# An attention block's output on one Trainium2 core: its second block by seven products, its loads ahead of the row sums' load, a fourth tile of the last head added by DMA

## The chip, the cores and the metric

The kernel runs on one core of one Trainium2 chip. The metric is the device time of one execution in microseconds; below 2% the comparison is made on medians of repeated runs. One execution was recorded by the hardware profiler.

## The reference

The inputs are one sequence of 2048 tokens of 1024 numbers (float32). Two branches see the same x and are mixed by a gate per token:

```python
qkv = (x @ wqkv).reshape(B, S, 3, H, Dh).transpose(2, 0, 3, 1, 4)   # H = 32, Dh = 32
scores = einsum("bhqd,bhkd->bhqk", q, k) * Dh ** -0.5
o = einsum("bhqk,bhkd->bhqd", softmax(scores), v)
a = o.transpose(0, 2, 1, 3).reshape(B, S, D) @ wo                    # S = 2048, D = 1024
b = ...            # experts picked by top-1 of two key tables, 64 experts, mixed by act * v
out = g * a + (1 - g) * b,    g = sigmoid((x * gate_w).sum(-1))
```

## The kernel before

The program first makes Q and K (kept in DRAM), the second branch's activations (ATD) and V. Then a loop runs over the 32 heads, 16 key tiles each. For a pair of key tiles TensorE makes the scores into a ring of PSUM banks (`scores`, L1322), ScalarE takes their exponentials into tiles P of 128 x 2048 (L1332), and TensorE multiplies the pair before with V (`pv`, L1343).

**Row sums.** The softmax needs the sum of P over all keys. `presum` adds the 16 tiles of a head: most of them by VectorE into ACC (L1370, L1372), some by DMA: one tile is written straight into ACCD, and others are added to it by an accumulating DMA on POOL's queue (L1365). `SUMS` names these key tiles; the first number is the tile that becomes ACCD. `merge` (L1375) adds ACCD to ACC. For the last head, number 31, tiles 14 and 15 are added by nobody: `rowsum` multiplies each with ones on TensorE (L1356), together with ACC, into one PSUM bank. That merge is planned at key tile 13 of the last head, ahead of the sum of tile 13.

**Normalisation.** `norm_sums` copies the sums out of PSUM and sends them to DRAM (SMD). `load_r` brings the sums of four heads back as a tile rr; `norm_r` takes the reciprocal, multiplies with the gate G64 and sends the factors to DRAM (RD). `load_rb` broadcasts them to 128 partitions (RB). `load_o` brings the unnormalised output of the heads (OD) as a tile V. Chunk 7 of each block, that is heads 28 to 31, has to wait for this chain behind the last head; chunks 0 to 6 have their factors before.

**Output.** It is made in 8 blocks of 256 tokens, each with four PSUM banks of 128 x 512. Every operand is split into a high and a low half, and three of the four half products are made. Blocks 0 and 1 are done plainly: `wo_mm` (L1525) makes 8 chunks of 12 matmuls, and `av_mm` (L1532) adds the second branch with 8 matmuls. Blocks 2 to 7 go through `unit`: seven products P1 to P7 of 12 matmuls each (L965) after Strassen and Winograd, on sums of the activations (S1 to S4, made by VectorE at L947 and split at L95 and L96) and sums of the weights (T1 to T4, prepared early and held in DRAM as TD). `load_t(i)` brings T(i+1); `Halves.operand` makes and splits one operand, `scale_o` applies the factors (L1579), `split_o` does so for the plain path (L1594), `plain_out` copies four banks and stores them.

**What sets the order.** The program is written out by hand and each engine runs its own list in order: a waiting instruction holds everything behind it on its engine or queue. The plain loads and stores are issued by SP (all from L77), the accumulating ones by POOL. Buffers are shared by name: z0, z1, wo_raw, acc, accd and V are taken again when their last reader is through. Block 0 starts with chunk 0 right behind the last head, then come the row sums, then chunks 1 to 7.

```python
1602 wo_mm(pa, 0, [0], True, False)
1603 finish(H - 1)
1604 sm = pso.tile([128, 512], F32, name="o")
1605 list(rowsum(sm, *(P[H - 1, NT - i] for i in (1, 2)), ACC.pop(H - 1)))
```

Of the kernel before, what the change touches and what calls it, by code (L numbers as in the profile page):

```python
# [16 lines left out]
S = 2048  # L17
D = 1024
H = 32
# [12 lines left out]
def gated_mha_peer_kernel(ctx, tc, xT, wqkv, wv, wo, wq, k12, ug, v, out):  # L32
# [42 lines left out]
    def dma(dst, src, queue=nc.sync):  # L75
        a, b = (ap.bitcast(F32) if ap.dtype == F32R else ap for ap in (dst, src))
        return queue.dma_start(a, b)  # L77
# [1270 lines left out]

    SUMS = (1, 3, 8, 12), (2, 4, 6)

    def rowsum(ps, *srcs):
        for src in srcs:
            for qc in range(NQ):
                yield nc.tensor.matmul(ps[32 * qc:32 * qc + 32, :], ones,  # L1356
                                       src[:, qc * 512:(qc + 1) * 512],
                                       start=(src is srcs[0]), stop=(src is srcs[-1]))

    def presum(h, kt):  # L1360
        sums = SUMS[h == H - 1]
        if kt == 0 or kt == sums[0] or (h == H - 1 and kt >= NT - 2):
            return
        if kt in sums:
            nc.gpsimd.dma_start(ACCD[h], P[h, kt], accum_op=OP.add)  # L1365
            return
        if kt == 1 + (sums[0] == 1):
            if h > 0:
                ACC[h] = wk.tile([128, S], F32, name="acc")
            nc.vector.tensor_add(ACC[h], P[h, 0], P[h, kt])  # L1370
        else:
            nc.vector.tensor_add(ACC[h], ACC[h], P[h, kt])  # L1372
# [10 lines left out]
    def finish(h):  # L1383
        g, j = divmod(h, 4)
        o = wk.tile([128, 512], F32, name="osb")
        nc.scalar.activation(o, O.pop(h), AF.Copy)
        dma(OD[:, :, j, :, g, :].rearrange("q d n s -> (q d) n s"),
            o.rearrange("p (n s) -> p n s", n=2))
# [14 lines left out]
    def norm_r(g):  # L1403
        r = R.pop(g)
        nc.vector.reciprocal(r, r)
        nc.vector.tensor_mul(r, r, G64)
        dma(RD[:, :, g, :].rearrange("j n (q m) -> (j n) q m", m=64), r)


    OC, RB = {}, {}  # L1410
# [13 lines left out]
    def load_chunk(n, k0, k1, queue=nc.sync):  # L1424
        load_o(n, k0, k1, queue)
        load_rb(n, k0, k1, queue=queue)
# [23 lines left out]
    def at(step, f, *a):  # L1450
        todo.setdefault(step, []).append((f, a))
# [14 lines left out]
            at(base + 7, load_v, g + 1, j)  # L1466
    for i, step in enumerate((6, 7, 9, 11)):
        at((H - 1) * NT + step, split_first, i)
    at((H - 1) * NT + 13, merge, H - 1)
    for k in range(2 * KC):  # L1470
        c = slice(k % 2 * D // 2, (k % 2 + 1) * D // 2)
        at((8 + k) * NT + 11, dma, raw_wo(k // 2)[:, c], wo_rows[:, :, k // 2 * D:(k // 2 + 1) * D][:, :, c])
# [9 lines left out]
    for b0 in range(0, (H + 1) * NT, BT):  # L1482
# [9 lines left out]
        for k in range(b0, b0 + BT):  # L1492
            for f, a in todo.pop(k, []):
                f(*a)
            if now:
                presum(*now[k - b0])
    assert not todo
    pss.close()
    pools["left"].close()
    pools["right"].close()  # L1500
# [15 lines left out]
    def load_at(n):  # L1516
        AT[n] = fin.tile([128, W], F32R, name="at", bufs=3)
        dma(AT[n], ATD[:, n * W:(n + 1) * W])
# [56 lines left out]
    def scale_o(n):  # L1575

        for k in range(2):
            o = OC[n][:, k * HC:(k + 1) * HC]
            nc.vector.tensor_mul(o, o, RB[n][:, k * HC:(k + 1) * HC])  # L1579
        ht.rows(OC[n])  # L1580
# [16 lines left out]
    def banks4():  # L1597
        return {(i, half): bank() for i in range(W // 128) for half in range(2)}
# [2 lines left out]
    pa = banks4()  # L1601
    wo_mm(pa, 0, [0], True, False)
    finish(H - 1)
    sm = pso.tile([128, 512], F32, name="o")
    list(rowsum(sm, *(P[H - 1, NT - i] for i in (1, 2)), ACC.pop(H - 1)))
    split_hi(1)
    for kc in range(1, KC - 1):
        split_hi(kc + 1)
        if kc == 1:
            norm_sums(H - 1, sm, nc.scalar)  # L1610
            load_r(G - 1)
            for n in range(2):
                load_at(n)
            load_o(1, 0, KC - 1)
            pso.close()
        split_lo(kc)
        wo_mm(pa, 0, [kc], False, False)
        if kc == HC:
            norm_r(G - 1)
    for n in range(2):  # L1620
        load_chunk(n, KC - 1, KC)
    load_rb(2, 0, KC)
    split_lo(KC - 1)
    split(woh[0], wol[0], raw_wo(0))

    load_t(2, None, [fin.tile([128, S], F32R, name="t3l")])
    OH[1] = zp.tile([128, KC, W], F32R, name="z1")
    OL[1] = wk.tile([128, KC, W], F32R, name="acc")  # L1630
    split_o(1, 0, HC)
    split_o(0, KC - 1, KC)
    load_o(2, 0, KC)
    load_t(0, *([keep.tile([128, S], F32R, name=f"wo_raw{j}")] for j in range(2)))
    ps_odd = Pool("ps_odd", space=PSUM)
    for (i, half), ps in pa.items():
        av_mm(0, i, half, ps)
    wo_mm(pa, 0, [KC - 1], False, True)
    split_o(1, HC, KC)
    load_at(2)  # L1640
    load_t(2, [zp.tile([128, S], F32R, name="z0")], None)
    load_t(1, *([keep.tile([128, S], F32R, name=f"wo_raw{2 + j}")] for j in range(2)))
    load_rb(3, 0, KC)
    load_o(3, 0, KC)
    pa1 = banks4()
    wo_mm(pa1, 1, list(range(KC - 1)), True, False)
    for (i, half), ps in pa1.items():
        av_mm(1, i, half, ps)
    plain_out(0, pa)
    load_t(3, *([part[k][:, 512:] for k in range(HC)] for part in (woh, wol)))  # L1650
    ht.places(wk.tile([128, S], F32R, name="acc"), "A11", "A12")
    ht.places(fin.tile([128, S], F32R, name="s31"), "S3", "S1")
    scale_o(2)
    for name in ("A11", "S3", "S1", "A12"):
        ht.operand(name)
    wo_mm(pa1, 1, [KC - 1], False, True)
    ht.places(zp.tile([128, S], F32R, name="z1"), "S2")
    ht.places(wk.tile([128, S], F32R, name="acc"), "S4", "A22")
    load_at(3)
    ht.b.update({f"B{i + 1}{j + 1}": [[part[i * HC + k][:, j * 512:(j + 1) * 512] for k in range(HC)]  # L1660
                                    for part in (woh, wol)] for i in range(2) for j in range(2)})

    def osb():
        return wk.tile([128, 512], F32, name="osb")

    def unit(n):
# [12 lines left out]

        p1 = ht.product("P1")  # L1680
        c1 = osb()
        nc.scalar.activation(c1, p1, AF.Copy)
        if n == 2:
            ht.operand("S2")
            plain_out(1, pa1)
            for name in ("S4", "A22"):
                ht.operand(name)
        if n + 2 < S // W:
            load_chunk(n + 2, 0, KC)
            load_at(n + 2)  # L1690
        ahead("A11")
        p7 = ht.product("P7")
# [10 lines left out]
        def c11():  # L1703
            p2 = ht.product("P2", lambda ps: av_mm(n, 0, 0, ps, first=True))
            pieces = 2 if last else 1
            for i in range(pieces):
                c = slice(i * 512 // pieces, (i + 1) * 512 // pieces)
                tt(c1[:, c], c1[:, c], p2[:, c])
                store(n, 0, 0, c1, c)
# [12 lines left out]
        def c21():  # L1722
            p4 = ht.product("P4", lambda ps: av_mm(n, 1, 0, ps, first=True))
            tt(u3, u3, p4)
            store(n, 1, 0, u3)

        if not last:
            c11()
# [12 lines left out]
    ps_even.close()  # L1741
    fin.close()
# [32 lines left out]
```

## Time and profile before

| | us |
|---|---|
| median of 3 runs | 1822.76 (1822.64 to 1823.33) |
| the profiled execution | 1822.43 |
| its span in the trace | 1820.6 |
| between the two, around the span | 1.8 |
| TensorE busy | 1813.5 |

The loop over heads ends near 1641 us after the span's start; from there the output runs to 1817. A line of the chain in order of time reads: start, duration, engine, tile, source line, number of instructions. A line of the timeline also names tiles and shapes, and in brackets the idle time before it with what ended it. A row of the windows gives, for a stretch, each engine's busy time and number of instructions, then the granted TensorE clock (1.00 is full), the share of the DMA engines' time and GB/s. In the page's last part the number behind the size is the median time from issue to landing. DVE is VectorE, ACT ScalarE, POOL GpSimd, SPq the queue that issues most transfers.

### The profile page before, as it was taken

The page shows a single profiled execution, that of the slowest core. Times are in us where ns is not written, and L with a number is a line of the kernel's source. Part 1 is how long each engine was busy: PE and PEld are TensorE (multiplying, and loading weights), DVE is VectorE, ACT ScalarE, POOL GpSimd, SP SyncE. Part 2 cuts the span into 40 slices and gives each one's busy share as a digit, 9 for nine tenths or more (in the row PEclk, how much of TensorE's full clock was granted, in tenths as well). Part 3 has the DMA queues.
Part 4 walks back from the last instruction along what each step waited for, and adds up shares of the span by engine and source line. Part 5 has one row for each costly group of instructions (what it writes and reads, how often), then busy time and mean ns, then how long its engine had stood idle before and what let it go on. Part 6 is the DMA issues. An engine that isn't in the chain of part 4 may idle for free.

```text
span 1820.6 us, 26391 instructions
## 1 busy us (share of the span) xinstructions
PE 1813.5 (100%) x10077; PEld 1100.2 (60%) x10077; DVE 1461.6 (80%) x1258; ACT 1313.0 (72%) x1716; POOL 227.7 (13%) x351
## 2 busy tenths in 40 slices
PE   9999999999999999999999999999999999999999
PEld 6777777788888644444444444444444444447887
DVE  8865966789967888888888888888888888897674
ACT  6545544522333699999999999999999999994221
POOL 1222222244101100000000000000000000000000
PEclk9999999999999999999999999999999999999999
DMA  7888698660267778777778878888787778866641
GB/s 272 281 276 273 216 295 289 196 220 13 81 231 247 223 166 183 156 170 165 169 171 174 185 160 179 171 172 181 164 185 167 163 164 181 186 149 240 256 157 58
DMA packets 117072, 345.23 MB, mean 190 GB/s; under 512 B 16112, under 2 KB 49552, under 8 KB 96016
## 3 DMA queue, kind: packets, MB, share of 16 engines
q1 hardware_dynamic: 87752, 196.35, 36.6%
q0 software_dynamic: 27888, 145.00, 34.5%
q10 hardware_dynamic: 1304, 2.17, 0.3%
q8 instruction: 80, 1.31, 0.3%
q14 instruction: 48, 0.39, 0.1%
HBM read 171.76 MB, written 72.36 MB: 134 GB/s over the span
## 4 chain that ended last, share of the span: by engine, by line
PE 99%; DMA 0%; ACT 0%; SPq 0%; DVE 0%; issue 0%; DVEq 0%; ACTq 0%
PE ring L1322 29%; PE o L1343 26%; PE bk L303 15%; PE pa L965 6%; PE bk L965 6%; PE bk L726 5%; PE pa L1525 2%; PE bk L984 2%; PE bk L291 2%; PE bk L342 2%; PE ring L1356 1%; PE pa L1532 1%; PE bk L191 0%; DMA xh<-in_xT 0%; PE bk L359 0%; ACT P L1332 0%
## 5 line engine op out<-in xcount | busy, mean ns | idle before, releaser
L1332 ACT ACTIVATE P<-ring 128x1024 f32<-128x1024 f32 (+2 forms) x1031 | 913.0, 984 | 13.3 <-DMA accd<-P 0.2
L1372 DVE TENSOR_TENSOR acc<-acc,P 128x2048 f32<-128x2048 f32 x319 | 730.9, 2291 | 74.4 <-ACT P L1332 47.9
L1343 PE MATMUL o<-P,V 128*32 128x512 f32 x3840 | 464.9, 599 | 0.0
L1322 PE MATMUL ring<-Q,K 98*128 98x512 f32 x1024 | 271.8, 407 | 0.1
L1322 PE MATMUL ring<-z,z 98*128 98x512 f32 x1020 | 270.5, 407 | 0.6 <-ACT accd L1332 0.6
L1322 PEld LDWEIGHTS ring<-Q,K 98*128 98x128 f32 x1024 | 182.4, 188 | 143.5 <-ACT P L1332 73.6
L1322 PEld LDWEIGHTS ring<-z,z 98*128 98x128 f32 x1020 | 181.7, 188 | 142.1 <-ACT P L1332 72.3
L1343 PEld LDWEIGHTS o<-P,V 128*32 128x32 f32 x3840 | 99.2, 109 | 223.1 <-issue 214.4
L1365 POOL DMA_DIRECT2D accd<-P x95 | 81.5, 858 | 928.6 <-ACT P L1332 349.5
L1370 DVE TENSOR_TENSOR acc<-P,P 128x2048 f32<-128x2048 f32 x32 | 73.4, 2292 | 72.9 <-ACT P L1332 72.9
L303 PE MATMUL bk<-xh,A 128*128 128x512 f32 x336 | 82.8, 396 | 0.0
L303 PE MATMUL bk<-xh,S 128*128 128x512 f32 x336 | 81.3, 393 | 0.0
L303 PE MATMUL bk<-xl,S 128*128 128x512 f32 x336 | 80.1, 391 | 0.0
L136 ACT ACTIVATE hi<-u 128x512 fp32r<-128x512 f32 x42 | 26.6, 632 | 71.5 <-issue 37.0
L303 PEld LDWEIGHTS bk<-xh,A 128*128 128x128 f32 x336 | 62.1, 188 | 23.7 <-issue 5.9
L1375 DVE TENSOR_TENSOR acc<-acc,accd 128x2048 f32<-128x2048 f32 x32 | 73.1, 2284 | 0.0
L303 PEld LDWEIGHTS bk<-xl,S 128*128 128x128 f32 x336 | 62.8, 188 | 16.2 <-issue 2.5
L303 PEld LDWEIGHTS bk<-xh,S 128*128 128x128 f32 x336 | 62.5, 188 | 14.5 <-issue 1.7
L1332 ACT ACTIVATE accd<-ring 128x1024 f32<-128x1024 f32 (+2 forms) x64 | 62.3, 1034 | 1.8 <-PE ring L1322 1.7
L965 PE MATMUL pa<-woh,acc 128*128 128x512 f32 x192 | 62.2, 390 | 0.0
L513 DVE TENSOR_TENSOR u<-u,bk 128x512 f32<-128x512 f32 x70 | 46.6, 682 | 10.5 <-DMA wpd<-u 6.2
L730 ACT ACTIVATE xu<-bk 128x64 f32<-128x64 f32 x16 | 3.6, 222 | 61.4 <-PE bk L726 61.4
(303 smaller groups left out, 2208.5 us busy)
## 6 DMA issues: line engine op xcount, KB each, us to landing
accd<-P POOLq DMA_DIRECT2D x95, 1024.0 KB, 7.8
wqt<-in_wq SPq DMA_DIRECT2D x64, 512.0 KB
wraw<-in_wqkv SPq DMA_DIRECT2D x28, 512.0 KB
kdh<-hi POOLq DMA_DIRECT2D x32, 256.0 KB, 6.2
kdl<-lo POOLq DMA_DIRECT2D x32, 256.0 KB, 6.7
qdh<-hi POOLq DMA_DIRECT2D x32, 256.0 KB, 6.1
qdl<-lo POOLq DMA_DIRECT2D x32, 256.0 KB, 5.9
z<-kdh SPq DMA_DIRECT2D x32, 256.0 KB
```

The source lines that it names most:

```text
L291: nc.tensor.matmul(b0[w, n], AW[PLAIN[w, ki]][a][:, k, :], X[f"B{ki + 1}{n + 1}"][b][:, k, :], start=first, stop=last)
L303: nc.tensor.matmul(ps, a[i][:, k, :], b[j][:, k, :], start=(k == 0 and i == j == 0), stop=(k == HC - 1 and i == 1))
L513: nc.vector.tensor_tensor(out=out, in0=a, in1=b, op=OP.add)
L726: nc.tensor.matmul(ps, x_part(a, t // 4, kc)[:, tok], b, start=first, stop=last)
L965: nc.tensor.matmul(ps, self.a[a][i][:, k, :], self.b[b][j][k], start=(not first and k == 0 and i == j == 0), stop=(k == HC - 1 and i == 1))
L1322: on_ring(nc.tensor.matmul(ring[:, i, :], K[:98, kt * 128:(kt + 1) * 128], Q[:98, qc * 512:(qc + 1) * 512], start=True, stop=True), i)
L1332: on_ring(nc.scalar.activation(P[h, kt][:, q0 * 512:(q0 + m) * 512].rearrange("p (a m) -> p a m", a=m), ring[:, i:i + m, :], AF.Exp, scale ...
L1343: nc.tensor.matmul(O[h][32 * qc:32 * qc + 32, :], Vt[g][:, kt, 32 * j:32 * j + 32], p[:, qc * 512:(qc + 1) * 512], start=(kt == 0), stop=( ...
L1365: nc.gpsimd.dma_start(ACCD[h], P[h, kt], accum_op=OP.add)
L1370: nc.vector.tensor_add(ACC[h], P[h, 0], P[h, kt])
L1372: nc.vector.tensor_add(ACC[h], ACC[h], P[h, kt])
L1375: nc.vector.tensor_add(ACC[h], ACC[h], ACCD[h])
```

## The change

Four things change, all behind key tile 10 of the last head.

1. `SUMS` of the last head gets a fourth tile, 11, that goes by DMA. `presum` leaves out only tile 15 now, so VectorE adds tile 14; `rowsum` multiplies tile 15 and ACC. The merge stands behind the loop.
2. Block 1 becomes a `unit` as blocks 2 to 7 are. Its P1 and P7 are made ahead of block 0's chunk 7; P2 comes right behind that. `plain_out(1, ...)` and block 1's split operands are gone.
3. SP's loads of block 1 and of T3 stand ahead of the load of the row sums (rr), T1 and T2 soon behind it.
4. The store of the last factors and the two small broadcasts of them (chunk 7 of blocks 0 and 1) move from SP's queue to POOL's.

```diff
-    SUMS = (1, 3, 8, 12), (2, 4, 6)
+    SUMS = (1, 3, 8, 12), (2, 4, 6, 11)
...
-        if kt == 0 or kt == sums[0] or (h == H - 1 and kt >= NT - 2):
+        if kt == 0 or kt == sums[0] or (h == H - 1 and kt == NT - 1):
             return
...
-    at((H - 1) * NT + 13, merge, H - 1)
...
     assert not todo
+    merge(H - 1)
...
     finish(H - 1)
+    for n in range(2):
+        load_at(n)
+    load_o(1, 0, KC - 1)
+    load_t(2, [zp.tile([128, S], F32R, name="z1")], [fin.tile([128, S], F32R, name="t3l")])
     sm = pso.tile([128, 512], F32, name="o")
-    list(rowsum(sm, *(P[H - 1, NT - i] for i in (1, 2)), ACC.pop(H - 1)))
+    list(rowsum(sm, P[H - 1, NT - 1], ACC.pop(H - 1)))
...
             for n in range(2):
-                load_at(n)
-            load_o(1, 0, KC - 1)
+                load_o(n, KC - 1, KC)
...
         if kc == HC:
-            norm_r(G - 1)
+            norm_r(G - 1, nc.gpsimd)
+            load_t(0, *([keep.tile([128, S], F32R, name=f"wo_raw{j}")] for j in range(2)))
     for n in range(2):
-        load_chunk(n, KC - 1, KC)
-    load_rb(2, 0, KC)
+        load_rb(n, KC - 1, KC, nc.gpsimd)
...
+    load_t(1, *([keep.tile([128, S], F32R, name=f"wo_raw{2 + j}")] for j in range(2)))
...
+    scale_o(1, 0)
+    for name in ("A11", "S3"):
+        ht.operand(name)
+    load_rb(2, 0, KC)
     split_o(0, KC - 1, KC)
     load_o(2, 0, KC)
...
     for (i, half), ps in pa.items():
         av_mm(0, i, half, ps)
+    early = ht.product("P1"), ht.product("P7")
     wo_mm(pa, 0, [KC - 1], False, True)
-    split_o(1, HC, KC)
+    scale_o(1, 1)
+    for name in ("A12", "S1"):
+        ht.operand(name)
...
-    pa1 = banks4()
-    wo_mm(pa1, 1, list(range(KC - 1)), True, False)
-    for (i, half), ps in pa1.items():
-        av_mm(1, i, half, ps)
     plain_out(0, pa)
     load_t(3, *([part[k][:, 512:] for k in range(HC)] for part in (woh, wol)))
...
-    for n in range(2, S // W):
-        unit(n)
+    for n in range(1, S // W):
+        unit(n, *(early if n == 1 else ()))
```

In `unit(1)` the operands S2, S4 and A22 are made behind the copy of P1, the product P2 and its sum come at once, and that sum goes to the fourth part of the tile `post` instead of the copy of P1.

What this does to SP's list, first before: from the store of the last head's output on (od), with rr the row sums, rd the factors, rb and accd the broadcast factors, V a block's heads, t0 to t3 the halves of T1 to T4.

```order
L77 DMA od<-osb 128x2x256
L77 DMA rr<-smd_80 128x64
L77 DMA at<-atd 128x256 x2
L77 DMA V<-od 128x1792
L77 DMA rd<-rr 32x4x64
L77 DMA V<-od 128x256
L77 DMA rb_5492<-rd 128x1x256
L77 DMA V<-od 128x256
L77 DMA accd<-rd 128x1x256
L77 DMA accd<-rd 128x1x2048
L77 DMA t3l<-t2l 128x2048
L77 DMA V<-od 128x2048
```

The same stretch of SP's list in the change:

```order
L77 DMA od<-osb 128x2x256
L77 DMA at<-atd 128x256 x2
L77 DMA V<-od 128x1792
L77 DMA z_12438<-t2h 128x2048
L77 DMA t3l<-t2l 128x2048
L77 DMA rr<-smd_80 128x64
L77 DMA V<-od 128x256 x2
L77 DMA wo_raw_12533<-t0h 128x2048
L77 DMA wo_raw_12534<-t0l 128x2048
L77 DMA wo_raw_12574<-t1h 128x2048
L77 DMA wo_raw_12575<-t1l 128x2048
L77 DMA accd<-rd 128x1x2048
```

The end of POOL's list in the change; before, it ended with its first row here:

```order
L1365 DMA accd<-P_12241 128x2048
L1365 DMA accd<-P_12315 128x2048
L77 DMA rd<-rr 32x4x64
L77 DMA rb_5492<-rd 128x1x256
L77 DMA accd<-rd 128x1x256
```

The row sums' load moved behind four loads, T1 and T2 moved ahead of block 2's loads, and the factors left SP's list for POOL's.

VectorE's last sums of the last head, before (P_12315 is key tile 11, P_12332 tile 12, P_12340 tile 13):

```order
L1372 TENSOR_TENSOR acc<-acc,P_12306 128x2048
L1446 TENSOR_TENSOR z_12263<-wo_raw_5490,z_12263 128x1024
L1446 TENSOR_TENSOR acc<-V,z_12264 128x256
L1372 TENSOR_TENSOR acc<-acc,P_12315 128x2048
L1372 TENSOR_TENSOR acc<-acc,P_12332 128x2048
L1375 TENSOR_TENSOR acc<-acc,accd 128x2048
L1372 TENSOR_TENSOR acc<-acc,P_12340 128x2048
```

and in the change (P_12356 is tile 14):

```order
L1372 TENSOR_TENSOR acc<-acc,P_12306 128x2048
L1446 TENSOR_TENSOR z_12263<-wo_raw_5490,z_12263 128x1024
L1446 TENSOR_TENSOR acc<-V,z_12264 128x256
L1372 TENSOR_TENSOR acc<-acc,P_12332 128x2048
L1372 TENSOR_TENSOR acc<-acc,P_12340 128x2048
L1372 TENSOR_TENSOR acc<-acc,P_12356 128x2048
L1375 TENSOR_TENSOR acc<-acc,accd 128x2048
```

Tile 11 is gone from VectorE's list, tile 14 has come, and the merge is the last of the four.

More of the change, by code (lines that the diff above doesn't have):

```diff
@@ L1401, in load_r, with norm_r @@
         dma(R[g], SMD[g].rearrange("j (b m) -> (j b) m", m=64))
-    def norm_r(g):
+    def norm_r(g, queue=nc.sync):
         r = R.pop(g)
@@ L1406, in norm_r @@
         nc.vector.tensor_mul(r, r, G64)
-        dma(RD[:, :, g, :].rearrange("j n (q m) -> (j n) q m", m=64), r)
+        dma(RD[:, :, g, :].rearrange("j n (q m) -> (j n) q m", m=64), r, queue)
     OC, RB = {}, {}
@@ L1573, in load_t, with scale_o @@
             ops[n] = [place[:, k * 512:(k + 1) * 512] for place in part for k in range(m)]
-    def scale_o(n):
-        for k in range(2):
+    def scale_o(n, *ks):
+        for k in ks or range(2):
             o = OC[n][:, k * HC:(k + 1) * HC]
@@ L1618, in gated_mha_peer_kernel @@
         if kc == HC:
-            norm_r(G - 1)
+            norm_r(G - 1, nc.gpsimd)
+            load_t(0, *([keep.tile([128, S], F32R, name=f"wo_raw{j}")] for j in range(2)))
     for n in range(2):
-        load_chunk(n, KC - 1, KC)
-    load_rb(2, 0, KC)
+        load_rb(n, KC - 1, KC, nc.gpsimd)
     split_lo(KC - 1)
     split(woh[0], wol[0], raw_wo(0))
[L1628 to L1631, printed above, removed]
+    load_t(1, *([keep.tile([128, S], F32R, name=f"wo_raw{2 + j}")] for j in range(2)))
+    ht.b.update({f"B{i + 1}{j + 1}": [[part[i * HC + k][:, j * 512:(j + 1) * 512] for k in range(HC)]
+                                    for part in (woh, wol)] for i in range(2) for j in range(2)})
+    ht.places(wk.tile([128, S], F32R, name="acc"), "A11", "A12")
+    ht.places(fin.tile([128, S], F32R, name="s31"), "S3", "S1")
+    scale_o(1, 0)
+    for name in ("A11", "S3"):
+        ht.operand(name)
+    load_rb(2, 0, KC)
     split_o(0, KC - 1, KC)
     load_o(2, 0, KC)
-    load_t(0, *([keep.tile([128, S], F32R, name=f"wo_raw{j}")] for j in range(2)))
     ps_odd = Pool("ps_odd", space=PSUM)
@@ L1637, in gated_mha_peer_kernel, with unit @@
         av_mm(0, i, half, ps)
+    early = ht.product("P1"), ht.product("P7")
     wo_mm(pa, 0, [KC - 1], False, True)
-    split_o(1, HC, KC)
+    scale_o(1, 1)
+    for name in ("A12", "S1"):
+        ht.operand(name)
     load_at(2)
[L1641 to L1644, printed above, removed]
-    pa1 = banks4()
-    wo_mm(pa1, 1, list(range(KC - 1)), True, False)
-    for (i, half), ps in pa1.items():
-        av_mm(1, i, half, ps)
     plain_out(0, pa)
     load_t(3, *([part[k][:, 512:] for k in range(HC)] for part in (woh, wol)))
[L1651 to L1657, printed above, removed]
+    ht.places(zp.tile([128, S], F32R, name="z0"), "S2")
     ht.places(wk.tile([128, S], F32R, name="acc"), "S4", "A22")
-    load_at(3)
-    ht.b.update({f"B{i + 1}{j + 1}": [[part[i * HC + k][:, j * 512:(j + 1) * 512] for k in range(HC)]
-                                    for part in (woh, wol)] for i in range(2) for j in range(2)})
     def osb():
         return wk.tile([128, 512], F32, name="osb")
-    def unit(n):
+    def unit(n, p1=None, p7=None):
         u2, u3, u5 = (post[:, i] for i in range(3))
@@ L1678, in ahead, with c11 @@
                 ht.operand(name)
-        p1 = ht.product("P1")
+        def c11():
+            p2 = ht.product("P2", lambda ps: av_mm(n, 0, 0, ps, first=True))
+            pieces = 2 if last else 1
+            r = post[:, 3] if n == 1 else c1
+            for i in range(pieces):
+                c = slice(i * 512 // pieces, (i + 1) * 512 // pieces)
+                tt(r[:, c], c1[:, c], p2[:, c])
+                store(n, 0, 0, r, c)
+        p1 = p1 or ht.product("P1")
         c1 = osb()
         nc.scalar.activation(c1, p1, AF.Copy)
[L1683 to L1686, printed above, removed]
+        if n == 1:
+            for name in ("S2", "S4", "A22"):
                 ht.operand(name)
@@ L1690, in unit @@
             load_at(n + 2)
+        if n == 1:
+            c11()
         ahead("A11")
-        p7 = ht.product("P7")
+        p7 = p7 or ht.product("P7")
         ahead("S3")
@@ L1701, in unit @@
         ahead("S2")
[L1703 to L1709, printed above, removed]
         def c12():
@@ L1727, in unit @@
         if not last:
-            c11()
+            if n > 1:
+                c11()
             ahead("A12")
```

## The prediction

> **What bounds the kernel now.** I read the page first: busy shares, then the chain that ended last.
>
> ```profile
> span 1820.6 us, 26391 instructions
> PE 1813.5 (100%) x10077; PEld 1100.2 (60%) x10077; DVE 1461.6 (80%) x1258; ACT 1313.0 (72%) x1716; POOL 227.7 (13%) x351
> PE 99%; DMA 0%; ACT 0%; SPq 0%; DVE 0%; issue 0%; DVEq 0%; ACTq 0%
> ```
>
> TensorE is the bound: 99% of the chain is its own work. So a matmul removed is worth its slot, if nothing that it covered comes late. Next, the chain in order of time, for the stretch that the change touches (start, us, what):
>
> ```profile
> 1627.21 0.86 PE ring L1356 x8
> ...
> 1641.50 2.95 PE pa L1525 x12
> 1644.45 2.71 PE o L1356 x24
> 1647.16 16.56 PE pa L1525 x72
> 1663.73 1.81 PE pa L1532 x8
> 1665.54 21.76 PE pa L1525 x96
> 1687.30 1.81 PE pa L1532 x8
> 1689.12 2.72 PE pa L1525 x12
> 1691.83 10.88 PE pa L965 x48
> ```
>
> From 1641.5 on TensorE never pauses: L1525 is the plain output matmuls, L1356 the row sums with ones, L1532 the mixed-in second branch, L965 the seven products. 96 matmuls take 21.76 us, so one is 0.2267; L965 goes at the same pace (48 in 10.88). One tile's row sums are 8 instructions, 0.86 us.
>
> **What leaves TensorE.** Block 1 had 96 plain matmuls (84 at L1525 and the 12 at 1689.12); seven products of 12 are 84. Twelve fewer: 12 x 0.2267 = 2.72 us. Its 8 matmuls at L1532 stay, spread over four products. The row sums of tile 14 go: 0.86 us. The sum is 3.58 us, if each operand arrives in time. New stations: row sums end 1646.3, block 0's chunks 1 to 6 end 1662.9, its L1532 1664.7, P1 1667.4, P7 1670.1, block 0's chunk 7 1672.8, P2 1676.0, P5 1678.7, P6 1681.5, P3 1684.6, P4 from 1685.5 to 1688.2, where block 2 begins.
>
> **The fourth tile by DMA, and the merge behind the loop.** VectorE's last sums, and the two POOL issues before:
>
> ```profile
> 1634.72 4.68 DVE L1372 TENSOR_TENSOR acc<-acc,P 128x2048 f32<-128x2048 f32 x2
> 1639.43 2.29 DVE L1375 TENSOR_TENSOR acc<-acc,accd 128x2048 f32<-128x2048 f32 x1
> 1641.83 2.29 DVE L1372 TENSOR_TENSOR acc<-acc,P 128x2048 f32<-128x2048 f32 x1
> 1618.79 0.86 POOL L1365 DMA_DIRECT2D accd<-P  x1 [11.71 <-ACT P L1332]
> 1626.17 0.86 POOL L1365 DMA_DIRECT2D accd<-P  x1 [6.53 <-DMA accd<-P]
> accd<-P POOLq DMA_DIRECT2D x95, 1024.0 KB, 7.8
> ```
>
> VectorE still does four operations of 2.29 us here; tile 14 takes 11's place, and the merge is last instead of last but one. Its end stays near 1644.1, and the ones matmuls of the sum need it only at 1645.4: 1.2 us of slack. The merge now waits for tile 11's transfer. That starts when tile 6's has landed (issued 1626.17; the one before took 7.4 us until its follower went, so 1633.6) and takes 7.4 to 7.8: 1641.0 to 1641.4, before 1641.8. It would have to last 9.4 us to reach TensorE, then 1:1. I cost it at nothing.
>
> **The loads sent ahead of the row sums' load.** Behind the row sums runs a chain of small transfers: sums out, sums in (rr), reciprocal, factors out (rd), factors broadcast (rb, accd), scaling.
>
> ```profile
> 1647.86 1.06 ACTq L77 DMA_DIRECT2D smd<-ssb  x1
> 1649.67 0.34 SPq L77 DMA_DIRECT2D rr<-smd  x1
> 1653.43 0.55 DVE L1405 RECIPROCAL rr<-rr 128x64 f32<-128x64 f32 x1
> 1654.49 1.22 DVE L1556 TENSOR_TENSOR wol<-wo_raw,woh 128x1024 fp32r<-128x1024 f32 x1
> 1658.57 1.22 DVE L96 TENSOR_TENSOR wol<-wo_raw,woh 128x1024 fp32r<-128x1024 f32 x1
> 1645.00:1647.00 2.00, 2.00 (x23) 0.39 (x12) 1.80 (x4) 1.16 (x2) 0.00 (x0) 1.00 0.00 0
> 1665.00:1667.00 2.00, 2.00 (x11) 1.65 (x10) 0.87 (x2) 1.06 (x1) 0.00 (x0) 1.00 1.01 426
> ```
>
> The last two rows are windows (last columns: DMA share, GB/s). The DMA engines stood idle at 1645, and run at 426 GB/s when loads queue. Now V of block 1 and both halves of T3 (0.92 + 1.05 + 1.05 MB) are queued there from 1643.5: 7.1 us, to about 1653 with the 1.8 that a small transfer takes (1647.86 to 1649.67). The early end: sums out land 0.86 earlier than before, and rr lands behind the loads, 1653.3. The late end: the sums themselves wait behind them, and rr lands 1.8 later, 1654.8. The reciprocal begins between these; I take 1654. What follows it on VectorE: chunk 5's wol ends 2.3 us on (1655.71 - 1653.43), and TensorE needs it at 1658.2 (second third of chunk 5); wol 0 ends 6.4 us on, and A11 is ready 2.6 later (one scaling 1.22, the two halves of the split), needed at 1665.1. So the reciprocal may begin as late as 1655.9: cost nothing, slack 1.1 to 2.6 us, then 1:1.
>
> **Factors on the POOL queue.** Before, SP issued them:
>
> ```profile
> 1654.26 0.60 SPq L77 DMA_DIRECT2D rd<-rr  x1
> 1657.69 0.54 SPq L77 DMA_DIRECT2D rb<-rd  x1
> 1663.19 0.42 DVE L1594 TENSOR_TENSOR V<-V,rb 128x256 f32<-128x256 f32 x1
> kdh<-hi POOLq DMA_DIRECT2D x32, 256.0 KB, 6.2
> kdl<-lo POOLq DMA_DIRECT2D x32, 256.0 KB, 6.7
> t0h<-xh POOLq DMA_DIRECT2D x4, 256.0 KB, 2.5
> ```
>
> No small POOL transfer stands beside such loads here; the nearest rows are 256 KB ones, 2.5 us at best and 6.2 to 6.7 median in stages with SP loads. T1 and T2 (4.2 MB, 9.9 us) now run on SP meanwhile, so I take 6.2. Reciprocal 1654.0, issue 1654.9, rd lands 1661.1, POOL resumes 0.5 later, rb lands 1667.8. Chunk 7 of block 0, moved behind P1 and P7 (5.44 us of cover), needs it 0.9 earlier than 1670.1: slack 1.4. Block 1's own factor comes some 0.6 later and serves A12 for P2 at 1673.3, 1.9 us of work later: slack 3. Ends: 2.5 each gives 1660.4; 7.8 each (the 1 MB median) 1671.0, 1.8 late.
>
> POOL has nothing else to issue then. On SP, behind its wait for the sums, stand the last chunks of blocks 0 and 1, T1 and T2: they have until P5 (1676.0) and P6, 20 us for 4.5 MB.
>
> The Trainium skill, page "DMA: Bandwidth & Descriptors", section "Issuing engines are not separate DMA queues", speaks against this move: transfers from all queues run on the same 16 DMA engines, and another queue saves only issue time. By it the factors would stand in line with T1 and T2 as on SP, 1654.9 + 9.9 + 1.8 = 1666.6 if rd's turn is hidden in that and some 1670 if not: a sum of 3.58 or 2.8. The rows here, 2.5 alone and 6.2 beside loads, bear it out as far as they go.
>
> **VectorE and ScalarE in block 1.** They take on products' operands and sums:
>
> ```profile
> L1579 DVE TENSOR_TENSOR V<-V,accd 128x1024 f32<-128x1024 f32 x10 | 11.8, 1217 | 0.0
> L96 DVE TENSOR_TENSOR acc<-V,acc 128x512 fp32r<-128x512 f32 x22 | 15.0, 688 | 5.4 <-ACT acc L95 5.2
> L95 ACT ACTIVATE acc<-V 128x512 fp32r<-128x512 f32 x22 | 13.6, 626 | 26.4 <-DVE V L947 16.5 <-PE pa L965 5.2 <-issue 4.8
> L947 DVE TENSOR_TENSOR ssb<-V 128x512 f32<-128x512 f32 x10 | 6.8, 684 | 0.0
> 1680.00:1685.00 5.00, 5.00 (x24) 4.15 (x23) 0.00 (x0) 0.00 (x0) 0.00 (x0) 1.00 1.03 433
> 1685.00:1690.00 5.00, 5.00 (x24) 4.15 (x23) 0.00 (x0) 0.00 (x0) 0.00 (x0) 1.00 0.99 403
> ```
>
> VectorE: 2 scalings, 4 sums, 7 low halves, 8 additions: 2.4 + 2.7 + 4.8 + 5.5 = 15.4 us, for 6.2 before (4 at 1.22, 2 copies of 0.68): 9.2 more. It was idle for all of 1680 to 1690, so this fits. Strung from the factor at 1668.4 with a ScalarE half (0.63) in each split, S2 is ready by 1677 (P6 at 1678.7), the reader that frees P7's bank ends near 1688.5 (wanted 1690.9). T4's eight loads start behind four stores, near 1675, and have 2.1 MB, 4.9 us: about 1683, for P4 at 1685.5. Nothing, with 2 us of slack.
>
> **Sum.** 2.72 + 0.86 + 0 = 3.58 us: 1822.43 becomes 1818.85 in the profiled execution. The median of the runs is 0.33 above that execution, so 1822.76 becomes **1819.2**.
>
> **Rivals.**
> (1) The factor comes late and chunk 7 waits for it. For it: three queues now meet on full DMA engines. Against: 1.4 us of slack and 5.44 of cover. It decides from 1669.2 on, 1:1; between 0.3 and 3.3 us late gives 1819.5 to 1822.5.
> (2) The other side: each POOL transfer waits out all of SP's backlog, rd behind T1, and rb behind T2 and block 2's factors (3.1 MB, 7.4 us), each with 1.8 to 2.5 of its own. At 10 us each rb lands 1675.4 and TensorE waits 6.2: 1822.43 - 3.58 + 6.2 + 0.33 = 1825.4; slower from 3.58 us of wait on, that is 8.7 us each.
> (3) No backlog is waited out: each small transfer waits at most for one load in flight, 2.5 us, and takes 1.8 to 2.5 itself. Then rr is early, rb lands by 1665 and all the slack stays: 1819.2 as in the forecast, with (1) and (2) excluded. The Trainium skill, same page, section "Queues, rings and completion order", has such a rule: a DMA engine alternates between queues by packets, typically of 9 to 17 descriptors. No row so far tells it from the forecast's 6.2.
> (4) Tile 11's transfer takes over 9.4 us, or VectorE's string slips by 2: 0.5 to 2 us, 1819.7 to 1821.2.
>
> **How the numbers follow.** Forecast 0.62, of which 0.2 by way of (3); (1) 0.22; (2) 0.10; (4) 0.06. The range 1818.7 to 1822.5 takes the forecast with 0.4 of scatter and all of (1) and (4). The bound of 0.2% (about what a measurement can tell from no change) is 3.65 us, and the forecast is 3.58: its chance splits in halves, so faster 0.31; same 0.60, with (1), (4) and a little of (2); slower 0.09.
>
> **What would show it.** Right: the chain stays on TensorE from 1641 on, block 2's first L965 begins near 1688.2, row sums are x16, no wait of TensorE beside them. (1) and (2) show as TensorE idle before L1525's last 12, VectorE waiting at L1594 for a DMA; (4) as VectorE waiting at L1375, or TensorE at P7 of block 2 or at P4. The forecast is wrong if any such wait exceeds 0.4 us, or the DMA share is not near 1 from 1645 to 1668.

## The result, and the profile after

| | before | change |
|---|---|---|
| median | 1823.35 us (12 runs, 1822.64 to 1825.73) | 1820.13 us (12 runs, 1819.35 to 1821.93) |
| ratio of the change to before | | 0.9982, 95% interval 0.9975 to 0.9990 |
| profiled execution, and its span | 1822.43, 1820.6 us | 1820.62, 1818.8 us |
| TensorE busy | 1813.5 us | 1810.3 us |

The change is 3.22 us faster by the medians; 3.58 was forecast, and the predicted 1819.2 lies 0.93 under the median. Of these 0.93, 0.59 is the kernel before: the three runs that were shown had 1822.76, all twelve have 1823.35. Repeated beside two experiments, the change gave 1819.02 (11 runs) against 1822.39, a ratio of 0.998 (0.9971 to 0.9989).

First the chain in order of time of the change (start, us, what), from the row sums of head 30 (L1356 into ring), which both kernels make alike, to the last twelve products:

```profile
1628.80 0.86 PE ring L1356 x8
...
1643.09 2.95 PE pa L1525 x12
1646.04 1.85 PE o L1356 x16
1647.90 16.59 PE pa L1525 x72
1664.48 1.81 PE pa L1532 x8
1666.30 5.44 PE pa L965 x24
1671.74 2.72 PE pa L1525 x12
1674.46 0.45 PE pa L1532 x2
1674.91 8.16 PE pa L965 x36
...
1686.24 0.91 PE pa L1532 x4
1687.15 13.60 PE pa L965 x60
...
1812.27 2.73 PE pa L965 x12
```

Everything here stands 1.59 us later than in the trace of before (1628.80 against 1627.21), although nothing was changed ahead of it. So places are compared after taking off 1.59. Row sums end at 1647.90 - 1.59 = 1646.31 (forecast 1646.3), block 0's mixing ends and P1 starts at 1664.71 (1664.7), chunk 7 starts at 1670.15 (1670.1), P2's mixing at 1672.87 (1672.8). P4 starts at 1685.56 (1685.5) and takes 2.72, so block 2 starts at 1688.28 (1688.2). TensorE does not wait once. In the kernel before, the row that answers to the last one is:

```profile
1814.23 2.73 PE pa L965 x12
```

From the first row to the last the kernel before takes 1814.23 - 1627.21 = 187.02 us and the change 1812.27 - 1628.80 = 183.47: 3.55 less, against 3.58 forecast. This stretch, within one trace, is the yardstick of all that follows, since whole executions scatter by more than the terms in question.

**Where the 1.59 us come from.** The windows at the start of the program (us, busy time and number of instructions of TensorE, weight loads, VectorE, ScalarE, GpSimd, then the granted clock), of the change and then of the kernel before:

```profile
8.00:10.00 2.00, 0.38 (x2) 0.00 (x0) 0.00 (x0) 0.49 (x1) 0.00 (x0) 1.00 0.95 313
12.00:14.00 2.00, 2.00 (x6) 1.52 (x6) 2.00 (x5) 1.64 (x4) 0.00 (x0) 0.50 1.04 408
```

```profile
8.00:10.00 2.00, 1.21 (x6) 0.67 (x4) 0.21 (x1) 0.88 (x2) 0.00 (x0) 1.00 0.94 312
12.00:14.00 2.00, 2.00 (x10) 1.64 (x9) 1.99 (x4) 1.65 (x4) 0.00 (x0) 1.00 1.04 407
```

In the profiled execution of the change TensorE was nearly idle from 8 to 10 us, waiting for the second chunk's operands, and its granted clock was 0.50 two microseconds later; the matmul behind its first 400 started at 81.35 us against 79.60, 1.75 late. The control run of the same kernel has that matmul at 79.16, and the same late start shows in two of the kernels below, so it is a scatter of the start, not of the change. Without it the profiled execution would have taken 1820.62 - 1.75 = 1818.87 us, where 1818.85 was forecast. That is an estimate; the control's own profiled execution took 1818.60.

**What answers to the other predicted steps.** VectorE's rows of the timeline (idle time before, and what ended it, in brackets):

```profile
1643.41 2.29 DVE L1375 TENSOR_TENSOR acc<-acc,accd 128x2048 f32<-128x2048 f32 x1
1656.48 0.56 DVE L1405 RECIPROCAL rr<-rr 128x64 f32<-128x64 f32 x1 [2.18 <-DMA rr<-smd]
1669.40 0.42 DVE L1594 TENSOR_TENSOR V<-V,rb 128x256 f32<-128x256 f32 x1 [2.04 <-DMA rb<-rd]
1670.31 0.42 DVE L96 TENSOR_TENSOR acc<-V,z 128x256 fp32r<-128x256 f32 x1 [0.48 <-ACT z L95]
1671.38 1.23 DVE L1579 TENSOR_TENSOR V<-V,accd 128x1024 f32<-128x1024 f32 x1 [0.64 <-DMA accd<-rd]
1673.30 0.69 DVE L96 TENSOR_TENSOR acc<-V,acc 128x512 fp32r<-128x512 f32 x1 [0.70 <-ACT acc L95]
```

The merge (L1375) waits for nothing. The reciprocal, block 0's last scaling (L1594) and block 1's second scaling (L1579) now each wait for a transfer. These waits are VectorE's, and TensorE has its operands in time: chunk 7's last half ends at 1670.73, and chunk 7 starts at 1671.74.

The issues: the row sums' store on ScalarE's queue, their load on SP's, and the factors on POOL's; then the medians from issue to landing:

```profile
1648.59 1.06 ACTq L77 DMA_DIRECT2D smd<-ssb  x1
```

```profile
1653.84 0.32 SPq L77 DMA_DIRECT2D rr<-smd  x1
```

```profile
1657.60 0.60 POOL L77 DMA_DIRECT2D rd<-rr  x1 [21.16 <-DVE rr L1406]
1663.30 0.55 POOL L77 DMA_DIRECT2D rb<-rd  x1 [5.10 <-DMA rd<-rr]
```

```profile
rb<-rd POOLq DMA_DIRECT2D x1, 128.0 KB, 6.1
accd<-rd POOLq DMA_DIRECT2D x1, 128.0 KB, 7.5
rd<-rr POOLq DMA_DIRECT2D x1, 32.0 KB, 5.4
```

### The profile page after: what moved, and what is told of

Its sections match the earlier page's. It is cut to its first block, busy times and chain, and to the rows that moved or that the text cites. A ratio compares the mean times of both kernels' runs of the same rounds, so it can differ in the third digit from the quotient of the medians.

```text
span 1818.8 us, 26381 instructions
## 1 busy us (share of the span) xinstructions
PE 1810.3 (100%) x10057; PEld 1096.5 (60%) x10057; DVE 1470.1 (81%) x1273; ACT 1314.7 (72%) x1720; POOL 230.7 (13%) x355
## 4 chain that ended last, share of the span: by engine, by line
PE 99%; DMA 0%; ACT 0%; SPq 0%; issue 0%; DVE 0%; DVEq 0%; ACTq 0%
PE ring L1322 29%; PE o L1343 26%; PE bk L303 15%; PE pa L965 7%; PE bk L965 6%; PE bk L726 5%; PE bk L291 2%; PE bk L984 2%; PE bk L342 2%; PE ring L1356 1%; PE pa L1525 1%; PE pa L1532 1%; PE bk L191 0%; DMA xh<-in_xT 0%; PE bk L359 0%; ACT P L1332 0%
## 5 line engine op out<-in xcount | busy, mean ns | idle before, releaser
L1375 DVE TENSOR_TENSOR acc<-acc,accd 128x2048 f32<-128x2048 f32 x32 | 73.1, 2284 | 0.0
L965 PE MATMUL pa<-woh,acc 128*128 128x512 f32 x224 | 72.5, 389 | 0.0
```

The costliest lines, as they stand in the source:

```text
L965: nc.tensor.matmul(ps, self.a[a][i][:, k, :], self.b[b][j][k], start=(not first and k == 0 and i == j == 0), stop=(k == HC - 1 and i == 1))
L1375: nc.vector.tensor_add(ACC[h], ACC[h], ACCD[h])
```

## The experiments

All kernels together. The stretch here runs from the first matmul of head 30's row sums to the start of the very last matmul, which is 2.5 us more than in the first four expectations (189.54 before, 185.98 in the change). Each ratio is to runs of the kernel before taken beside it (medians of 1822.39 to 1823.35).

| kernel | stretch, us | against before | median, us (runs) | ratio to before, 95% interval |
|---|---|---|---|---|
| before | 189.54 | | 1823.35 (12) | |
| the change | 185.98 | -3.56 | 1820.13 (12) | 0.9982 (0.9975 to 0.9990) |
| the change again | 185.97 | -3.57 | 1819.02 (11) | 0.998 (0.9971 to 0.9989) |
| row sums alone | 188.71 | -0.83 | 1821.93 (11) | 0.9994 (0.9985 to 1.0003) |
| all but the row sums | 186.91 | -2.63 | 1820.38 (11) | 0.9986 (0.9977 to 0.9995) |
| chunk 7 ahead of P1, P7 | 191.99 | +2.45 | 1826.64 (10) | 1.0019 (1.0010 to 1.0028) |
| rr's load first | 186.78 | -2.76 | 1819.67 (10) | 0.998 (0.9971 to 0.999) |
| factors on SP | 185.97 | -3.57 | 1818.83 (9) | 0.9979 (0.9969 to 0.9989) |
| T3 loaded twice | 188.61 | -0.93 | 1821.07 (1) | |
| T1 and T2 late | 190.40 | +0.86 | 1825.03 (10) | 1.0013 (1.0003 to 1.0022) |
| the same, nothing beside rb | 193.03 | +3.49 | 1825.98 (1) | |
| six small matmuls | 186.99 | -2.55 | 1819.84 (11) | 0.9984 (0.9975 to 0.9993) |
| these, and factors on SP | 185.97 | -3.57 | 1819.53 (11) | 0.9982 (0.9973 to 0.9991) |

The theory was that the time is TensorE's slots and everything else has slack. The main rival was that the factor's way is what counts.

**The row sums alone.**

```diff
-    SUMS = (1, 3, 8, 12), (2, 4, 6)
+    SUMS = (1, 3, 8, 12), (2, 4, 6, 11)
...
-    list(rowsum(sm, *(P[H - 1, NT - i] for i in (1, 2)), ACC.pop(H - 1)))
+    list(rowsum(sm, P[H - 1, NT - 1], ACC.pop(H - 1)))
```

> The kernel before with the fourth DMA tile (11), the merge behind the loop and one row-sum tile less; block 1 stays plain, loads and factors as before. The times of whole executions scatter by over 1 us, so each theory is put for the stretch of the chain that the change touches: from the start of the row sums of head 30 (L1356 into ring) to the start of the last 12 products (L965). It is 187.02 us in the kernel before (1627.21 to 1814.23) and 183.47 in the change (1628.80 to 1812.27). Theory (slots only): 8 instructions less, 0.86: 186.16. Rival (tile 11's transfer or the merge comes late): above 186.5, with VectorE waiting for a DMA at L1375. Second rival (the gain of the change lies in the products alone): 187.0. Median some 0.9 us below the kernel before, which five rounds hardly tell from nothing.

The chain of this kernel:

```profile
1628.76 0.86 PE ring L1356 x8
...
1646.00 1.85 PE o L1356 x16
...
1814.95 2.73 PE pa L965 x12
```

1814.95 - 1628.76 = 186.19, where 186.16 was expected: 0.83 us gained, and no wait for tile 11. The medians differ by 0.8 in the same direction, but the interval of their ratio includes 1, so they alone show no difference.

**The products without the row sums.** The same lines the other way round, in the change.

> The change without its first part: tile 14 goes back to the ones matmuls, tile 11 to VectorE, the merge to its old place; the seven products, the loads ahead and the factors on POOL stay. Theory (slots only): 12 x 0.2267 = 2.72 less than before: the stretch is 184.30. The row sums' chain starts 0.86 later, and so does all that needs it, so the slack stays. Rival (the two parts lean on each other: without the earlier row sums the factor comes late): above 184.6, with TensorE idle before block 0's last 12 at L1525. Median some 2.7 us below the kernel before.

```profile
1628.25 0.86 PE ring L1356 x8
...
1675.17 8.27 PE pa L965 x36
...
1812.64 2.73 PE pa L965 x12
```

184.39, expected 184.30. The row at 1675.17 is P2, P5 and P6: 36 matmuls in 8.27 us, not 8.16 as in the change. The waits between 1674 and 1684 name the reason, a weight load that waited for the low half of A12:

```profile
PEld pa L965 <- DVE acc L96: 0.2, 1, 0.2
```

So the two parts add up (0.83 + 2.63 = 3.46 of 3.56), and the second stands close to its limit at P2.

**The cover taken away.**

```diff
-    early = ht.product("P1"), ht.product("P7")
     wo_mm(pa, 0, [KC - 1], False, True)
+    early = ht.product("P1"), ht.product("P7")
```

> The change, with block 0's chunk 7 ahead of P1 and P7 of block 1 instead of behind them, so that these 5.44 us of TensorE work no longer cover the factor's way. In the change's trace block 0's mixing ends at 1666.30, and the first half that chunk 7 needs is there near 1670.3 (scaling at 1669.40, one ScalarE half). Theory (the cover carries the change): TensorE waits 1670.3 - 1666.3 = 4.0 us there, P1 and P7 follow without a wait, the stretch is 187.5 and the time slightly above the kernel before's. Rival (the factor's way is not what sets it; TensorE's order could be changed at no cost): 183.5.

The chain, and the granted clock (0.56 and 0.58) in the windows around it:

```profile
1663.61 5.93 DMA rb<-rd
...
1669.57 0.44 DVE V L1594
...
1670.49 4.49 PE pa L1525 x12
```

```profile
1670.00:1672.00 2.00, 1.51 (x4) 1.22 (x5) 0.78 (x2) 0.42 (x1) 0.00 (x0) 0.56 1.03 336
1672.00:1674.00 2.00, 2.00 (x7) 1.57 (x6) 1.30 (x2) 0.63 (x1) 0.00 (x0) 0.58 0.79 291
```

The chain leaves TensorE for the factor's transfer, and the whole gain is gone with more. The wait was 4.2 us, as expected (4.0). Not expected: the twelve matmuls behind it took 4.49 us and not 2.72, at a little over half the clock. Together 4.2 + 1.8 = 6.0 us, which is the 191.99 against 185.98. That P1 and P7 stand ahead of chunk 7 is what lets block 1's products be worth their slots.

**The row sums' load first.** The loads of block 1 and T3 moved back behind `load_r`.

> The change, with the row sums' load (rr) ahead of the loads of block 1 and T3 again, as in the kernel before. Theory (slots only, both orders have slack): the stretch stays 183.5; the row sums' store and load no longer meet loads, so the reciprocal does not wait for rr and begins 2.2 us earlier counted from the row sums; block 1's V and T3 land some 3 to 4 us later and still before P1 and P7. Rival (the early loads are needed ahead of rr): P1 or P7 waits, the stretch grows by 1 us or more, with TensorE idle before the first L965 or VectorE waiting at L1579 for V. Second rival (rr first makes the time shorter, since the factor was late): below 183.3.

The reciprocal waited for nothing, as expected. But the stretch grew by 0.8 us over the change's, neither at P1 nor at VectorE's wait for V. Two of the waits between 1680 and 1695:

```profile
DVE rb L971 <- DMA out<-rb: 3.1, 1, 3.1
PE pa L965 <- DVE rb L971: 0.4, 1, 0.4
```

The loads now stand some microseconds later in SP's queue, and block 0's stores stand behind them. VectorE's sum u2 (L971) goes into the place that such a store still reads, waits 3.1 us for it, and what hangs on VectorE's list comes late for P7 of block 2: its first matmul starts 0.6 us late, at 1691.71. So the early loads are worth 0.8 us, and it shows some 40 us behind them. The first theory (both orders have slack) and the rival (P1 or P7 of block 1 waits) both missed the place. The median does not show it, since executions scatter by more.

**The factors on SP's queue.**

```diff
-            norm_r(G - 1, nc.gpsimd)
+            norm_r(G - 1)
...
-        load_rb(n, KC - 1, KC, nc.gpsimd)
+        load_rb(n, KC - 1, KC)
```

> The change, with the store of the last factors (rd) and their two small broadcasts (rb, accd) back on SP's queue; everything else as in the change. In the change's trace rd is issued by POOL 1.1 us after the reciprocal's start and lets the broadcasts go 5.7 us later, and the scaling that waits for rb begins 6.1 us after that. SP's queue gives its transfers in the order of issue, so here rd goes ahead of T1 (landed in about 2 us), T1's halves follow, and rb stands behind them: about 5 us for T1 and 1.5 of its own. Theory (the time is TensorE's slots as long as the factor's way fits under P1 and P7): factor some 4 us earlier than in the change, stretch from the row sums of head 30 to the last product 186.0 by the start of the very last matmul (185.98 in the change, 189.54 before), no difference in time. Rival (POOL's queue is what makes the order possible; on SP the factors or T1 and T2 behind them are late): TensorE idle before block 0's last 12 or before P5 or P6, stretch over 187.

The rows of VectorE, in this trace 2.13 us earlier than in the change's (head 30's row sums start at 1626.49 and 1628.62):

```profile
1653.93 0.55 DVE L1405 RECIPROCAL rr<-rr 128x64 f32<-128x64 f32 x1 [1.78 <-DMA rr<-smd]
1664.72 0.42 DVE L1594 TENSOR_TENSOR V<-V,rb 128x256 f32<-128x256 f32 x1
```

From the reciprocal to the scaling are 10.8 us here and 12.9 in the change, and the scaling no longer waits for its factor. The stretch is the same, 185.97. So the move to POOL's queue brought nothing, and cost at least 2.1 us of slack.

**More in SP's queue, and less.** Three kernels. In the first T3 is loaded a second time behind T1:

```diff
             load_t(0, *([keep.tile([128, S], F32R, name=f"wo_raw{j}")] for j in range(2)))
+            load_t(2, *t3)
```

> The change, with both halves of T3 loaded a second time to the same place, on SP's queue right behind T1's two halves: 2.1 MB more (4.9 us at 426 GB/s) that stands in SP's queue when POOL issues rd. The result is the same. Theory A (a small transfer on POOL's queue waits out what SP has issued before it): rd takes 5 us longer than the 5.4 of the change, rb follows behind T2 and is 4 to 6 us later than in the change, and TensorE waits 3 us or more before block 0's last 12. Theory B (it waits for a bounded share of the loads only, whatever stands behind): rd and rb take 5.4 and 6.1 us as in the change, TensorE does not wait, stretch 186.0.

In the second T1 and T2 are loaded behind block 2's heads, in the third block 2's factors as well (the third is shown, without the lines at the old places of T1 and T2):

```diff
-    load_rb(2, 0, KC)
     split_o(0, KC - 1, KC)
     load_o(2, 0, KC)
+    load_rb(2, 0, KC)
+    load_t(0, *([keep.tile([128, S], F32R, name=f"wo_raw{j}")] for j in range(2)))
+    load_t(1, *([keep.tile([128, S], F32R, name=f"wo_raw{2 + j}")] for j in range(2)))
```

> The change, with the loads of T1 and T2 moved behind the load of block 2's heads, so that SP has nothing in its queue when POOL issues rd, and only block 2's factors (1 MB) when it issues rb. Both theories of the queues: rd takes 2 to 2.5 us from issue to landing instead of 5.4, rb 2 to 4.5 instead of 6.1; the scaling that waits for rb begins 4 to 6 us earlier, counted from the reciprocal. A value above 4 for rd would mean that the transfer is slow by itself and not by its neighbours. T1 and T2 are issued some 12 us later; T1 is wanted by P5 10 us after the mixing of block 0, T2 by P6 2.7 us later, and 5.2 MB stand ahead of T2's end (12 us): TensorE may wait 0 to 3 us at P5 or P6. Stretch (to the very last matmul's start) 186 to 189.

> As the kernel with T1 and T2 late, and with the 1 MB broadcast of block 2's factors moved behind the load of block 2's heads as well: now nothing stands on SP's queue when POOL issues rd, and nothing when it issues rb. With T1 and T2 late alone, rd took 1.86 us from issue to landing (5.41 in the change), and rb still 5.79 with that broadcast beside it. Theory (a small transfer on POOL's queue is slow by what runs beside it): rb lands 2 to 2.5 us after its issue. Rival (the broadcast of 128 rows is slow by itself on POOL's queue): 5 to 6 us again. The time itself is not of interest: T1 and T2 stay late, TensorE waits at P5 and P6, and at block 2's products.

From issue to landing on POOL's queue, in us:

| | rd, 32 KB | rb, 128 KB |
|---|---|---|
| 2.1 MB more in SP's queue | 5.3 | 6.4 |
| the change | 5.4 | 6.1 |
| T1 and T2 late | 1.9 | 5.8 |
| the same, block 2's factors late too | 1.9 | 3.7 |

So rd is slow by its neighbours, but not by how many stand in line: 4.9 us more of backlog (2.1 MB at 426 GB/s) add nothing, while the kernels with these loads beside rd scatter from 4.9 to 5.9 us. That excludes the theory that a POOL transfer waits out all of SP's queue. For rb neither expectation of the last kernel held: 3.7 us lies between 2.5 and 5; a part is its own, and its twin for block 1 still runs beside it.

The first two kernels lost time elsewhere. With T3 twice, P7 waited for the second copy and P4 for T4, which the expectation had missed; with T1 and T2 late, P5 and P6 waited for them, 3.5 us together where 0 to 3 had been expected. The waits of TensorE, of the first and of the second kernel:

```profile
PE pa L965 <- DMA t3l<-t2l: 1.3, 1, 1.3
PE pa L965 <- DMA wol<-t3l: 0.2, 1, 0.2
```

```profile
PE pa L965 <- DMA wo_raw<-t1l: 2.5, 1, 2.5
PE pa L965 <- DMA wo_raw<-t0l: 1.0, 1, 1.0
```

**The scatter at the start.** The change again, and with small matmuls in the gap at 8 to 10 us:

```diff
+        if kc == 0:
+            fill = bank_at(3)
+            for i in range(6):
+                nc.tensor.matmul(fill[:, :128], ident, ident, start=True, stop=True)
```

> The changed kernel itself, again, as the control beside the two kernels that follow. Expected: median 1819.5 to 1820.2, some executions 1.5 to 2 us above the fastest ones. The stretch from the row sums of head 30 to the last product's start 185.98 again, whatever the total is.

> The change, with six small matmuls (ident with ident, 128 x 128, into a PSUM bank that nobody reads yet) at the start of the program, behind the first chunk's twelve matmuls, where TensorE waits for the second chunk's operands between 8 and 10 us. In the profiles so far TensorE was busy for 0.38 (the change), 0.44 and 0.51 us of these 2 us in three executions, and in these the granted clock fell to 0.50 between 12 and 14 and the 400th matmul stood at 81.3; in six others (0.53 to 1.97 us busy) the clock stayed at 1.00 and the matmul stood at 79.1 to 80.5. Theory (the wait lowers the clock, and this is the scatter of over 1.5 us between executions): with the gap filled the clock stays at 1.00, the 400th matmul stands at 79.1 to 79.8, the slow executions go, and the median falls by 0.3 to 1 us against the control. Rival (the clock falls for another reason): the same scatter as the control.

> The change with the factors on SP's queue and the six small matmuls together: the version that the runs so far point to. By the theory the stretch is 185.97 as with the factors on SP, and the start is as in the kernel with the small matmuls: the same median as that one, 0.3 to 1 us below the control and 3.5 to 4.5 us below the kernel before. Rival: one of them loses here, and the median is that of the control or above.

The clock stayed at 1.00 in all three profiles, the control's too, so these do not tell the theory from the rival. The start did not get shorter: counting off the twelve added instructions, the same matmul stands at 79.74 and 79.41 us, against 79.16 in the control. The medians are 0.8 and 0.5 above it. The small matmuls are not worth keeping, and no version was faster than the change clear of the scatter.

The kernel with the small matmuls lost 1.0 us in the stretch in its profiled execution. Its P4 waited (lines are 4 higher here): first VectorE's merge, then TensorE's wait, and the chain's row for the last of T4's low halves:

```profile
1642.69 2.29 DVE L1379 TENSOR_TENSOR acc<-acc,accd 128x2048 f32<-128x2048 f32 x1 [0.47 <-DMA accd<-P]
```

```profile
PE pa L969 <- DMA wol<-t3l: 0.7, 1, 0.7
```

```profile
1681.54 7.39 DMA wol<-t3l
```

These operands are the change's own, only the execution is another. How much later T4's last half came there is seen in the packets. T4's halves travel in packets of 2 KB, and the loads issued behind them in packets of 8 KB. From 1688 to 1689 the kernel with the small matmuls (second row) still moves small packets, and the change (first row) moves none:

```profile
DMA packets 50, 0.41 MB, mean 410 GB/s; under 512 B 0, under 2 KB 0, under 8 KB 0
DMA packets 58, 0.44 MB, mean 440 GB/s; under 512 B 2, under 2 KB 2, under 8 KB 5
```

The last small packet of T4 stands 0.85 us earlier in the change (1687.64 against 1688.49). So its last half landed near 1688.93 - 0.85 = 1688.1 there, by estimate.

## Why the prediction was right, step by step

**The slots** (3.58): right. The stretch lost 3.56 us, 0.83 and 2.63 when each part is alone, and nothing came late in the profiled executions of the change and of the control.

**The merge** (nothing, 1.2 us of slack to TensorE): right. It ended at 1645.70, and TensorE began with its sum at 1646.86. In the two executions with the small matmuls it waited 0.47 and 0.44 us for tile 11, and TensorE did not stop beside it. Rival (4) reached VectorE only.

**The reciprocal** (1654, between 1653.3 and 1654.8): 1656.48 - 1.59 = 1654.89, just behind the late end and 0.9 behind the value taken. The sums' store did wait among the loads, as the late end has it: from its issue to rr's issue it was 5.25 us (1648.59 to 1653.84), against 1.81 before. That is 1652.25 on the scale of before. From rr's issue to the reciprocal it was then 2.64 us, where 1.8 had been counted. The prediction's own terms (1643.5 + 7.1 + 1.8) give 1652.4, so its two ends hold 0.9 us that it does not name; by those terms the late end is 1654.2. With rr first again, VectorE does not wait there at all.

**The factor** (rb at 1667.8, 1.4 us of slack): the scaling began at 1669.40 - 1.59 = 1667.81. The hit is luck, since two misses of the same size cancelled: rd was issued 1.1 us later than forecast (1656.0), and let rb go after 5.7 us (1657.60 to 1663.30), not 6.7; rb took 6.1, near the 6.2. The slack for chunk 7 was 1.0 (1670.73 to 1671.74).

**Block 1's factor** (slack 3): too kind. It landed 7.5 us after its issue, the scaling began at 1669.79 on the scale of before, 1.4 later than forecast, and A12's low half was there at 1673.99, where P2's second matmul stands near 1675.1 and loads its weights 0.19 ahead: about 1.0 us. Without the earlier row sums this margin was overrun by 0.11.

**T4's loads** (landed by about 1683, slack 2): mis-sized, and the slack held for a reason that the prediction does not count. The loads were issued from 1676.9 on the scale of before, not near 1675, and the last landed near 1688.1 - 1.59 = 1686.5, so they took some 9.6 us and not 4.9, and the end is about 1 us behind P4's start. But P4 wants this last half only at its eleventh matmul, at 1687.15 + 10 x 0.2267 = 1689.42 in the change's trace. That leaves about 1.3 us. In the kernel with the small matmuls it was overrun by 0.9.

**VectorE's list** (P7's bank free at 1688.5, 2.4 us before block 2 wants it): nearly right. The sum that reads it (L971) ended at 1690.69 - 1.59 = 1689.1, which leaves 1.9.

**The rivals.** (2) is excluded, by the 2.1 MB that added nothing to rd. (3) has the right form, a bounded wait, but not its size: it was 5.4 and 6.1, not at most 4.3 to 5 (2.5 + 1.8 to 2.5 + 2.5). What the Trainium skill states on page "DMA: Bandwidth & Descriptors", section "Queues, rings and completion order", that an engine alternates between queues by packets, agrees with that: rd's 5.3 and 5.4 do not grow with the backlog, and fall to 1.9 when nothing runs beside it. (1) did not happen, but taking the cover away made it happen, at 1:1 and 1.8 us for the clock on top. The rule of the Trainium skill, same page, section "Issuing engines are not separate DMA queues", that another issuing queue saves issue time only, was cited against the move; the runs go further, since with SP's own queue the scaling came 2.1 us earlier.

**In sum.** The forecast held because each late transfer still had a little room: 1.0, 1.0 and about 1.3 us, where 1.4, 3 and 2 had been counted. That the medians show 3.22 and not 3.56 lies within the interval (1.8 to 4.6 us); whether single executions of the change lose part of a microsecond at P4, as the one with the small matmuls did, stays open.

## What to carry to other kernels

Where TensorE is 99% of the chain, count removed matmuls at their measured slot, and spend the work on the margins of what must land under them. One store beside a burst of loads (5.25 us for 1.8) made the reciprocal begin at 1654.89, where it had begun at 1653.43 before; the prediction had worked out 1655.9 as its limit. A reordering of TensorE's own list can be worth more than the arithmetic it makes room for: here 6.0 us against 2.7. Compare two traces between the same two instructions, not by their spans, when the parts in question are smaller than the scatter of the start.

## What the runs showed of the hardware that was not expected

**The clock can fall after short waits.** Three profiled executions had TensorE busy for 0.38, 0.44 and 0.51 of the two microseconds from 8 to 10, and all three had the granted clock at 0.50 from 12 to 14; with 0.53 us and more it stayed at 1.00 in the other ten. The waits themselves were 1.80, 1.56 and 1.49 us long, with pauses of 0.35 to 0.50 us some 3 us earlier. A wait of 4.2 us in the middle of the program cost 1.8 us more by the clock. The Trainium skill, page "TensorE: Matmul & The Clock Gate", section "What's actually happening", puts the fall to half at an idle window of about 3.4 us; the half agrees, but here a fall followed a wait of 1.5 to 1.8 us in three executions, and the measurement decides. The length of the wait alone does not decide: with T1 and T2 late, TensorE waited 1.47 us at the start and 2.5 us for T2, near 1680.6, and the granted clock stayed at 1.00 (the windows' third column from the right):

```profile
1678.00:1682.00 4.00, 2.38 (x11) 1.62 (x9) 0.23 (x1) 0.00 (x0) 0.00 (x0) 1.00 0.99 366
1682.00:1686.00 4.00, 3.13 (x14) 2.56 (x15) 0.00 (x0) 0.00 (x0) 0.00 (x0) 1.00 1.03 386
```

The small matmuls were to test the cause, and the control's clock did not fall either, so what else decides stays open.

**A small transfer on another queue did not wait out the backlog.** 32 KB on POOL's queue took 1.9 us with SP's queue empty, 5.4 beside loads and 5.3 beside loads with twice the backlog. On SP's own queue, issued ahead of the loads, it let its follower go after 2.2 us (1654.78 to 1656.95), against 5.7 on POOL's.
